# Batch 0's V turned by DMA, unit 0's scores in two PSUM homes, and loads held back, in an attention and SwiGLU kernel

## The chip, the cores and the metric

The kernel runs on one core of one Trainium2 chip. The metric is the device time of one launch in microseconds. The kernel before takes 279.68 us in the median of three runs (278.46 to 279.77).

## The reference

Four batches, eight heads, 768 tokens, head width 64. Tokens lie in eight blocks of 96. A matrix of 8 x 8 for each head (from five rounds of row and column normalization of `sort_net`) mixes the blocks of K and V; each block of queries then attends to its mixed block of keys alone. The result of all heads, 3072 x 512, goes through a SwiGLU feed-forward block with 1536 inner columns.

```python
for _ in range(5):                      # P: 8 x 8 for each head
    P = np.exp(P - np.max(P, axis=-1, keepdims=True))
    P = P / (np.sum(P, axis=-1, keepdims=True) + 1e-09)
    P = P / (np.sum(P, axis=-2, keepdims=True) + 1e-09)
k_sorted = np.einsum('bhij,bhjcd->bhicd', P, k_b)     # v_sorted alike
scores = scale * np.matmul(q_b, k_sb.transpose(0, 1, 2, 4, 3))
attn = softmax(scores)
x = np.matmul(attn, v_sb)               # then to (tokens, 512)
g = x @ w_gate
out = (g * sigmoid(g) * (x @ w_val)) @ w_out
```

## The kernel before, in words

The work is cut into eight units; unit u is half of a batch (four blocks of 96 tokens, `UT` = 384 tokens, all heads). Heads are taken in four pairs, `hp` 0 to 3, whose two heads (`x`) lie in the upper and lower 64 partitions.

Attention of a unit and a pair has eight steps: `qk` (scores into the PSUM home `s`), `rowmax` and `shift` (DVE reads the scores from PSUM; `shift` writes `e` to SBUF and frees `s`), `expo` (ACT), `rowsum` (DVE), `norm` (mostly POOL, writes `en`), `turn` (eight TensorE transposes of 96 x 96 and one eviction `et`), and `av` (matmuls with V, evicted by ACT to `xt`). The feed-forward of a unit has 12 columns of 128, m = 0 to 11: `ffn_up` computes gate `g_ps` and value `u_ps` with four matmuls each and the tanh on ACT, `ffn_gate` makes `gs` and the product `h` on DVE, and `ffn_down` of the unit before runs in between. For unit 0 every third product (m = 2, 5, 8, 11) is made by POOL from a copy `u_sb` that ACT makes.

PSUM homes are named by tag: `up` has three buffers, `o` one, `s` one of two banks, `m` two.

The order on each engine is written out by hand. Steps before the first feed-forward are called one after the other from the list `first`; all later steps are entered by `at(t, f, ...)` with a due time t (one unit of time is one column m of the feed-forward, so unit u's feed-forward begins at 12u, and T0 = -15.6 is unit 0's start), sorted by t and called in that order. Engines take their instructions strictly in the order of the calls, and each DMA queue too: loads are issued by POOL, so a load stands in POOL's order between its arithmetic; stores and DMA transposes are issued by SP.

K and V are mixed on TensorE by a block matrix `bdk` made from P. For K this gives the transposed form that `qk` wants (`mix_t`, six pieces, evicted to `kt`). V of batches 1 to 3 is mixed in natural form and goes through DRAM to its token-major form (`v_piece`, `v_turn`). For batch 0 V is mixed as K is, into `vT` (six `v0_piece`, L169), and then turned by TensorE: `v0_turn` (L176) makes four transposes of 128 x 96 into `vt_ps` and ACT evicts them to `vt`. One call covers one pair and one half of the blocks: half 0 (unit 0's blocks) is called in `first`, half 1 (unit 1's) in the due times 0.2 to 0.8.

The loads stand at these places of POOL's order: q, k, v of batch 0 and the first halves of the gate and value weights at the start; V and K of batch 1 ahead of the first mixing; the second halves of both weights and Q of batch 1 behind the making of `bdk`; the output weights at 0.1; V, K and Q of batch 2 at 2.1, 5.1 and 10.1 (Q in eight issues, `load_q_tok`).

## Time and profile before

| | |
|---|---|
| median of three runs | 279.68 us |
| the profiled execution, its own time | 279.93 us |
| its span, first to last instruction | 278.1 us |
| mean granted TensorE clock | 0.985 |
| TensorE busy | 253.2 us, 91% |
| DVE busy | 203.8 us, 73% |
| ACT busy | 146.8 us, 53% |
| POOL busy | 81.7 us, 29% |
| DMA, bytes moved | 30.27 MB |

All durations come from that one execution, so sums are made against 279.93; 1.8 us of it lie outside the span. A row of the timeline reads: start, duration, engine, line, operation, output and inputs, count, and in brackets the idle time before it with what ended it. A row of the chain of waits is a start, a length and what the chain ran through: an engine's work, or "issue", in which the engine waited for nothing that the profile shows. L129 and L131 are the lines of the helper `evict` on ACT and DVE, so such rows are told apart by their tiles. Names: `s` scores, `rm` maxima, `e` exponents, `rs` sums, `en` normalized, `et` turned, `vt` V with tokens in the partitions, `vm` mixed V of batch 1, `th` tanh.

### The profile page before, as it was taken

The numbers are of one execution on the slowest core, as the hardware profiler recorded it, in microseconds if no ns is written. First come the engines' busy times: TensorE is split into PE (matmuls) and PEld (weight loads), VectorE is DVE, ScalarE is ACT, GpSimd is POOL, SyncE is SP. The second block draws the span as 40 slices with busy tenths as digits, with TensorE's granted clock in tenths as the row PEclk, the third lists the DMA queues.
The fourth block names the chain that finished last, engine by engine and source line by source line (L and its number), as shares of the span: only waits on it lengthen the run. The fifth ranks groups of instructions, "written<-read, shape, count | busy, mean of one in ns | idle before, by whom it ended". The sixth has DMA issues, their size and how long they took to land.

```text
span 278.1 us, 5850 instructions
## 1 busy us (share of the span) xinstructions
PE 253.2 (91%) x2326; PEld 145.2 (52%) x2326; DVE 203.8 (73%) x362; ACT 146.8 (53%) x268; POOL 81.7 (29%) x114
## 2 busy tenths in 40 slices
PE   0586769998999999999999999999999999999973
PEld 0575643665555565555555555555555555555531
DVE  4679771886977877788887788888888887555500
ACT  2467665897665775755446554434444444333211
POOL 8255351437638422222222222222222222000000
PEclk9999995999999999999999999999999999999998
DMA  5999999989969994295221323343212221200111
GB/s 103 220 202 221 206 207 185 248 154 125 70 118 253 151 162 88 66 197 80 62 72 33 58 64 94 58 97 94 69 33 72 73 72 35 81 11 27 40 75 75
DMA packets 59611, 30.27 MB, mean 109 GB/s; under 512 B 51008, under 2 KB 54592, under 8 KB 59584
## 3 DMA queue, kind: packets, MB, share of 16 engines
q0 software_dynamic: 17968, 14.16, 33.6%
q1 hardware_dynamic: 41616, 15.74, 26.2%
q8 instruction: 18, 0.29, 0.4%
q14 instruction: 9, 0.07, 0.1%
HBM read 30.68 MB, written 8.65 MB: 141 GB/s over the span
## 4 chain that ended last, share of the span: by engine, by line
PE 81%; DVE 7%; ACT 6%; DMA 2%; issue 2%; DVEq 0%; ACTq 0%; POOLq 0%
PE o_ps L380 24%; PE u_ps L352 22%; PE g_ps L352 21%; PE av_ps L332 3%; PE k_ps L158 3%; PE s L275 3%; DMA qn<-in_q_dram 2%; DVE e L286 2%; DVE rm L281 2%; PE v_ps L188 2%; PE et_ps L319 2%; ACT e L291 1%; DVE rs L295 1%; ACT o_sb L384 1%; PE q_ps L139 1%
## 5 line engine op out<-in xcount | busy, mean ns | idle before, releaser
L352 PE MATMUL u_ps<-xt,wv_sb 128*128 128x384 bf16 x384 | 79.4, 330 | 1.0 <-DVE gs L366 0.9
L352 PE MATMUL g_ps<-xt,wg_sb 128*128 128x384 bf16 x384 | 80.0, 332 | 0.0
L366 DVE SCALAR_TENSOR_TENSOR gs<-th,g_ps 128x384 bf16<-128x384 bf16 x96 | 51.7, 539 | 37.9 <-ACT th L362 37.9
L362 ACT ACTIVATE th<-g_ps 128x384 bf16<-128x384 f32 x96 | 47.2, 492 | 59.6 <-PE g_ps L352 58.1
L380 PE MATMUL o_ps<-wo_sb,h 128*128 128x512 bf16 x288 | 76.8, 380 | 2.0 <-ACT o_sb L384 2.0
L372 DVE SCALAR_TENSOR_TENSOR h<-u_ps,gs 128x384 bf16<-128x384 f32 x92 | 51.3, 558 | 10.0 <-DVE gs L366 0.5
L352 PEld LDWEIGHTS <-wg_sb 128*128 128x128 bf16 x384 | 37.3, 99 | 35.3 <-issue 2.7
L352 PEld LDWEIGHTS <-wv_sb 128*128 128x128 bf16 x384 | 37.9, 99 | 28.6 <-issue 5.2
L306 POOL TENSOR_TENSOR enp<-e,rs 96x384 bf16<-96x384 f32 x32 | 25.7, 822 | 85.3 <-ACT xt L129 51.9
L306 POOL TENSOR_TENSOR en<-e,rs 96x384 bf16<-96x384 f32 x30 | 24.9, 847 | 46.6 <-DVE rs L296 41.8
L291 ACT ACTIVATE e<-e 96x768 f32<-96x768 f32 x32 | 27.1, 846 | 20.7 <-DVE e L286 20.6
L380 PEld LDWEIGHTS <-h 128*128 128x128 bf16 x288 | 24.6, 98 | 24.2 <-issue 3.1
L286 DVE TENSOR_TENSOR e<-s,rm 96x768 f32<-96x768 f32 x32 | 30.5, 953 | 2.8
L281 DVE TENSOR_REDUCE rm<-s 96x8 f32<-96x768 f32 x32 | 30.1, 942 | 1.4 <-PE s L275 1.4
L295 DVE TENSOR_REDUCE rs<-e 96x8 f32<-96x768 f32 x32 | 30.0, 938 | 1.3 <-ACT e L291 1.3
L384 ACT COPY o_sb<-o_ps 128x512 f32<-128x512 f32 x24 | 14.0, 583 | 16.7 <-PE o_ps L380 16.7
L129 ACT CAST xt<-av_ps 128x384 bf16<-128x384 f32 x32 | 15.3, 480 | 9.6 <-PE av_ps L332 9.6
L129 ACT CAST kt<-k_ps 128x512 bf16<-128x512 f32 x21 | 12.3, 585 | 5.6 <-PE k_ps L158 5.5
L332 PEld LDWEIGHTS <-vt 96*64 96x64 bf16 x256 | 8.3, 116 | 11.3 <-issue 10.6
L129 ACT CAST vm<-v_ps 128x512 bf16<-128x512 f32 x18 | 10.4, 590 | 4.1 <-PE v_ps L188 3.9
L101 POOL DMA_DIRECT2D qk<-in_q_dram x16 | 12.4, 784 | 0.0
L129 ACT COPY et<-et_ps 96x768 bf16<-96x768 bf16 x15 | 11.8, 786 | 0.8 <-PE et_ps L319 0.8
(61 smaller groups left out, 161.5 us busy)
## 6 DMA issues: line engine op xcount, KB each, us to landing
out_dram<-o_sb SPq DMA_DIRECT2D x24, 256.0 KB, 2.1
kn<-in_k_dram POOLq DMA_DIRECT2D x4, 768.0 KB, 10.4
vn<-in_v_dram POOLq DMA_DIRECT2D x4, 768.0 KB, 12.6
vscr<-vm SPq DMA_DIRECT2D x3, 768.0 KB, 6.2
vt<-vscr SPq DMA_DIRECT2D x3, 768.0 KB, 10.3
qn<-in_q_dram POOLq DMA_DIRECT2D x2, 768.0 KB, 13.5
wg_sb<-in_moe_w_gate_dram POOLq DMA_DIRECT2D x4, 384.0 KB, 15.4
wv_sb<-in_moe_w_val_dram POOLq DMA_DIRECT2D x4, 384.0 KB, 17.8
```

The lines of the kernel that those rows point to most:

```text
L129: nc.scalar.copy(dst, src)
L281: nc.vector.reduce_max(m[:, :, :, 0], st["s", u, hp], axis=AX.X)
L286: nc.vector.tensor_tensor(e, st["s", u, hp], st["m", u, hp].to_broadcast([BLK, 2, HB, BLK]), op=ALU.subtract)
L291: nc.scalar.activation(st["e", u, hp], st["e", u, hp], AF.Exp, scale=scale)
L295: nc.vector.reduce_sum(rs[:, :, :, 0], st["e", u, hp], axis=AX.X)
L306: engs[x].tensor_tensor(st["en", u, hp][:, x], st["e", u, hp][:, x], st["rs", u, hp][:, x].to_broadcast([BLK, HB, BLK]), op=ALU.mult)
L352: nc.tensor.matmul(ps, lhsT=w_sb[:, kc, ts(m, 128)], rhs=xt[u][:, kc, :], start=(kc == 0), stop=(kc == HP - 1))
L362: nc.scalar.activation(st["th"], st["g"], AF.Tanh, scale=0.5)
L366: nc.vector.scalar_tensor_tensor(gs, st["th"], 1.0, st["g"], op0=ALU.add, op1=ALU.mult)
L372: nc.vector.scalar_tensor_tensor(h_t[u][:, m, :], st["u"], 0.5, gs, op0=ALU.mult, op1=ALU.mult)
L380: nc.tensor.matmul(st["o"], lhsT=h_t[u][:, m, ts(t, 128)], rhs=wo_sb[:, m, :], start=(m == 0), stop=(m == NFC - 1))
L384: nc.scalar.copy(o_sb, st["o"])
```

## The change

Five things are changed.

V of batch 0 is turned by four DMA transposes on SP's queue, one for each pair and for both halves, each from 128 x 1024 columns of `vT` to 128 x 8 x 128. For that `vT` is padded from 96 to 128 columns a block, and POOL sets the pad to zero. All calls of the old `v0_turn` are gone, those in the due times too, and `av` reads V through `v_block`. The `v0_piece` results go through the PSUM homes `m` and `o` in place of `up`.

In unit 0 the scores of pairs 1 and 3 go into two one-bank tiles of `up` rather than the two-bank `s`; their `rowmax` and `shift` are then two instructions each. `qk` of pairs 1 and 2 is called one step earlier, that of pair 3 behind the turn of pair 0.

The loads of V and K of batch 1 are called behind the second normalization of unit 0, those of the second weight halves and of Q of batch 1 behind the fourth.

The first `rowmax` of unit 1 is given the due time T0 + 12.25 = -3.35 (before -3.5), which puts it behind the turn of unit 0's pair 3 (-3.4), whose eviction is DVE's.

In unit 0's feed-forward POOL makes the products of m = 2, 5, 9, 11 rather than 2, 5, 8, 11.

```diff
--- before.py
+++ after.py
@@ -158,8 +158,8 @@
                 nc.tensor.matmul(ps[ds(64 * x, 64), l, :], lhsT=nat[:, n * 8 + l, :],
                                  rhs=bdk[:, b, ds(HP * x, HP)].rearrange("p a i c -> p (a i c)"),
                                  start=True, stop=True)
-        dst = dst.rearrange("p hp i (ch c) -> p (hp i ch) c", ch=CH)
-        evict(eng, dst[:, :, ts(n, 8)], ps.transpose([0, 2, 1]))
+        dst = dst.rearrange("p hp i (ch c) -> p (hp i) ch c", ch=CH)
+        evict(eng, dst[:, :, :, ts(n, 8)], ps.rearrange("p c (hi ch) -> p hi ch c", ch=CH))
 
     def k_piece(b, n, eng, tag):
         if n == 0:
@@ -168,18 +168,23 @@
 
     def v0_piece(n, eng, tag):
 
+
         if n == 0:
-            tr["vT"] = natp.tile([128, HP, NB, BLK], BF16, name="vT", tag="vm", bufs=2)
-            tr["v", 0] = trp.tile([BLK, H * NB, D], BF16, name="vt", tag="vt", bufs=3)
-        mix_t(vn[0], 0, tr["vT"], n, eng, tag)
-
-    def v0_turn(hp, half, eng, tag):
-        ps = ps_tile([BLK, HB, 2, D], BF16, "vt_ps", tag)
-        for i in range(HB):
-            nc.tensor.transpose(ps[:, i].rearrange("p x d -> p (x d)"),
-                                tr["vT"][:, hp, half * HB + i, :], ident)
-        dst = tr["v", 0].rearrange("p (x hp i) d -> p hp i x d", x=2, hp=HP)
-        evict(eng, dst[:, hp, ds(half * HB, HB)], ps)
+            tr["vT"] = natp.tile([128, HP, NB, 128], BF16, name="vT", tag="vm", bufs=2)
+            tr["vt0"] = trp.tile([128, HP, NB, 2 * D], BF16, name="vt", tag="vt", bufs=3)
+            nc.gpsimd.memset(tr["vT"][:, :, :, BLK:], 0.0)
+        mix_t(vn[0], 0, tr["vT"][:, :, :, 0:BLK], n, eng, tag)
+
+    def v0_turn():
+        for hp in range(HP):
+            nc.sync.dma_start_transpose(out=tr["vt0"][:, hp],
+                                        in_=tr["vT"][:, hp].rearrange("p i k -> p (i k)"))
+
+    def v_block(b, x, hp, i):
+
+        if b == 0:
+            return tr["vt0"][0:BLK, hp, i, ds(D * x, D)]
+        return tr["v", b][:, (x * HP + hp) * NB + i, :]
 
     def v_piece(b, n, eng, tag):
         if n == 0:
@@ -268,23 +273,34 @@
 
     def qk(u, hp):
         b, i0 = u // 2, (u % 2) * HB
-        s = ps_tile([BLK, 2, 512], FP32, "s", "s")
+        if u == 0 and hp % 2:
+            s = [ps_tile([BLK, 1, 512], FP32, "s", "up") for x in range(2)]
+            parts = [(ds(x, 1), s[x]) for x in range(2)]
+            s = [s[x][:, 0] for x in range(2)]
+        else:
+            both = ps_tile([BLK, 2, 512], FP32, "s", "s")
+            parts = [(ds(0, 2), both)]
+            s = [both[:, x] for x in range(2)]
         for i in range(HB):
             for x in range(2):
                 r = ds(64 * x, 64)
-                nc.tensor.matmul(s[:, x, ts(i, BLK)], lhsT=tr["q", b][r, hp, i0 + i, :],
+                nc.tensor.matmul(s[x][:, ts(i, BLK)], lhsT=tr["q", b][r, hp, i0 + i, :],
                                  rhs=tr["k", b][r, hp, i0 + i, :], start=True, stop=True)
-        st["s", u, hp] = s[:, :, 0:UT].rearrange("p x (i k) -> p x i k", i=HB)
+        st["s", u, hp] = [(xs, p[:, :, 0:UT].rearrange("p x (i k) -> p x i k", i=HB))
+                          for xs, p in parts]
 
     def rowmax(u, hp):
         m = smp.tile([BLK, 2, HB, 1], FP32, name="rm", tag="rm")
-        nc.vector.reduce_max(m[:, :, :, 0], st["s", u, hp], axis=AX.X)
+        for xs, s in st["s", u, hp]:
+            nc.vector.reduce_max(m[:, xs, :, 0], s, axis=AX.X)
         st["m", u, hp] = m
 
     def shift(u, hp):
         e = epool.tile([BLK, 2, HB, BLK], FP32, name="e", tag="e", bufs=3)
-        nc.vector.tensor_tensor(e, st["s", u, hp],
-                                st["m", u, hp].to_broadcast([BLK, 2, HB, BLK]), op=ALU.subtract)
+        for xs, s in st["s", u, hp]:
+            m = st["m", u, hp][:, xs]
+            nc.vector.tensor_tensor(e[:, xs], s, m.to_broadcast([BLK, m.shape[1], HB, BLK]),
+                                    op=ALU.subtract)
         st["e", u, hp] = e
 
     def expo(u, hp):
@@ -330,7 +346,7 @@
         for i in range(HB):
             for x in range(2):
                 nc.tensor.matmul(ps[ds(64 * x, 64), i, :],
-                                 lhsT=tr["v", b][:, (x * HP + hp) * NB + i0 + i, :],
+                                 lhsT=v_block(b, x, hp, i0 + i),
                                  rhs=st["et", u, hp][:, x, i, :], start=True, stop=True)
         evict("act", xt[u][:, hp, :].rearrange("p (i q) -> p i q", i=HB), ps)
 
@@ -364,7 +380,7 @@
     def ffn_gate(u, m):
         gs = gsp.tile([128, UT], BF16, name="gs", tag="gs")
         nc.vector.scalar_tensor_tensor(gs, st["th"], 1.0, st["g"], op0=ALU.add, op1=ALU.mult)
-        if u == 0 and m % 3 == 2:
+        if u == 0 and m in (2, 5, 9, 11):
             u_sb = gsp.tile([128, UT], FP32, name="u_sb", tag="u_sb", bufs=2)
             nc.scalar.activation(u_sb, st["u"], AF.Copy, scale=0.5)
             nc.gpsimd.tensor_tensor(h_t[u][:, m, :], u_sb, gs, op=ALU.mult)
@@ -410,8 +426,6 @@
         at(tv[-1] + 0.3, v_turn, b)
 
     T0 = -15.6
-    load_v(1)
-    load_k(1)
     zk_ps = spread_p(0, 1), spread_p(1, B)
     make_zk(0, 1, zk_ps[0])
     make_bdk(0, nc.vector)
@@ -420,33 +434,31 @@
     make_zk(1, B, zk_ps[1])
     for b in range(1, B):
         make_bdk(b, nc.gpsimd)
-    load_w(wg_sb, moe_w_gate, DF // 2, DF)
-    load_w(wv_sb, moe_w_val, DF // 2, DF)
-    load_q(1)
 
 
     def v0(*ns):
         for n in ns:
-            v0_piece(n, "act", "up")
-
-    def vx(half, *hps):
-        for hp in hps:
-            v0_turn(hp, half, "act", "up")
-
-    first = [(qk, 0), (rowmax, 0), (v0, 0, 1, 2), (shift, 0), (expo, 0), (qk, 1), (rowmax, 1),
-             (v0, 3, 4), (shift, 1), (expo, 1), (v0, 5), (rowsum, 0), (norm, 0), (qk, 2),
-             (rowmax, 2), (vx, 0, 0, 1), (shift, 2), (expo, 2), (rowsum, 1), (norm, 1),
-             (vx, 0, 2, 3), (qk, 3), (turn, 0), (rowmax, 3), (shift, 3), (expo, 3), (av, 0),
-             (turn, 1), (rowsum, 2), (norm, 2, (nc.gpsimd, nc.vector)), (av, 1), (rowsum, 3),
-             (norm, 3, (nc.vector, nc.gpsimd))]
+            v0_piece(n, "act", ("m", "o", "m")[n % 3])
+
+    def loads(*fs):
+        for f, *args in fs:
+            f(*args)
+
+    half = DF // 2
+    first = [(qk, 0), (rowmax, 0), (v0, 0, 1, 2), (qk, 1), (shift, 0), (expo, 0), (rowmax, 1),
+             (v0, 3, 4), (qk, 2), (shift, 1), (expo, 1), (v0, 5), (v0_turn,), (rowsum, 0), (norm, 0),
+             (rowmax, 2), (shift, 2), (expo, 2), (turn, 0), (rowsum, 1), (norm, 1),
+             (loads, (load_v, 1), (load_k, 1)), (qk, 3), (av, 0), (rowmax, 3), (shift, 3), (expo, 3),
+             (turn, 1), (rowsum, 2), (norm, 2, (nc.gpsimd, nc.vector)),
+             (av, 1), (rowsum, 3), (norm, 3, (nc.vector, nc.gpsimd)),
+             (loads, (load_w, wg_sb, moe_w_gate, half, DF), (load_w, wv_sb, moe_w_val, half, DF),
+              (load_q, 1))]
     for f, *args in first:
-        f(*args) if f in (v0, vx) else f(0, *args)
+        f(*args) if f in (v0, v0_turn, loads) else f(0, *args)
     at(T0 + 11.9, turn, 0, 2)
     at(T0 + 12.2, turn, 0, 3, "dve")
     at(T0 + 12.3, av, 0, 2)
     at(T0 + 12.6, av, 0, 3)
-    for hp in range(HP):
-        at(0.2 + 0.2 * hp, v0_turn, hp, 1, "act", "o")
 
     at(0.1, load_wo)
     at(2.1, load_v, 2)
@@ -463,6 +475,8 @@
              [(26.6, 50.6)[b - 2] + (1, 3)[b - 2] * n for n in range(4)], "m")
     for u in range(1, NU):
         steps += att_steps(u, 12 * u + T0 + (u == 2))
+        if u == 1:
+            steps[-8 * HP + 1] = (T0 + 12.25, steps[-8 * HP + 1][1])
     for u in range(NU):
         for m in range(NFC):
             at(12 * u + m, ffn_up, u, m)
```

## The prediction

> **What bounds the kernel now.** First the page's slices: TensorE is full from slice 7 on, so what comes after about 50 us is a chain of matmuls that only shifts. The loss is in front of it, with one slice of low granted clock.
>
> ```profile
> PE   0586769998999999999999999999999999999973
> PEclk9999995999999999999999999999999999999998
> ```
>
> Next the busy time by stage (columns: PE, PEld, DVE, ACT, POOL busy, granted clock, DMA share, GB/s).
>
> ```profile
> 17.00:31.00 14.00, 10.01 (x183) 8.85 (x182) 12.63 (x18) 10.54 (x18) 9.06 (x14) 1.00 1.10 213
> 34.40:38.00 3.60, 3.21 (x15) 1.77 (x13) 2.63 (x4) 1.65 (x4) 1.42 (x2) 1.00 1.15 211
> 38.00:41.40 3.40, 1.39 (x18) 1.03 (x18) 2.37 (x5) 3.21 (x6) 1.94 (x3) 0.96 1.09 210
> 41.40:47.50 6.10, 5.43 (x25) 2.44 (x25) 1.11 (x2) 2.85 (x6) 1.46 (x3) 0.50 1.18 181
> 47.50:50.00 2.50, 2.50 (x20) 1.28 (x19) 1.17 (x2) 1.77 (x4) 0.46 (x1) 0.91 1.27 225
> ```
>
> From 17 to 31 (unit 0's attention) DVE is the full engine: 12.63 of 14.00. From 38.0 to 41.4 ACT is (3.21 of 3.40), TensorE works 1.39, and then its clock is 0.50 for six microseconds. The chain of waits says what ACT does there:
>
> ```profile
> 38.33 0.74 ACT e L291
> 39.08 0.56 ACT vt L129
> 39.64 0.70 ACT et L129
> 40.34 0.48 ACT vm L129
> 40.82 0.49 ACT vt L129
> ...
> 41.36 0.60 PE vt_ps L179 x4
> ...
> 41.98 0.59 ACT vt L129
> ...
> 42.61 0.58 PE v_ps L188
> 43.20 1.28 PE g_ps L352 x4
> 44.48 1.28 PE u_ps L352 x4
> ```
>
> The second half of V's turn (vt) alternates between TensorE and ACT in front of the second gate matmul. At 43.20 four gate matmuls take 1.28 us; at 49.76 they take 0.65.
>
> Last, the timeline of POOL where unit 2 begins:
>
> ```profile
> 64.12 0.91 POOL L370 TENSOR_TENSOR h<-u_sb,gs 128x384 bf16<-128x384 f32 x1 [2.06 <-DVE gs L366]
> 64.97 6.20 POOL L101 DMA_DIRECT2D qk<-in_q_dram  x8
> 71.18 0.93 POOL L370 TENSOR_TENSOR h<-u_sb,gs 128x384 bf16<-128x384 f32 x1
> 72.06 1.61 POOL L306 TENSOR_TENSOR en<-e,rs 96x384 bf16<-96x384 f32 x2
> 73.38 0.71 PE L319 MATMUL et_ps<-ident,en 96*96 96x96 bf16 x8
> ```
>
> Eight load issues hold POOL for 6.20 us, the product of m=11 and unit 2's first normalization follow without a gap, and TensorE's turn (73.38) stands at the second half of that normalization, done at 73.67.
>
> **A. Scores in two homes (unit 0, hp 1 and 3).** qk 1 no longer waits for shift 0 (end 19.06): it runs behind v0 pieces 0 to 2, so rowmax 1 starts at 19.10 instead of 19.72, -0.62. Against it, rowmax and shift of hp 1 and 3 become two instructions each, four extra. No row has 96x384 from PSUM on DVE; near rows are h (384 columns from PSUM, 558 ns) and e (768, 953 ns), so two halves cost 1.12 against 0.95: +0.16 each, +0.64 in all. The other end is +0.10 each, since an instruction that needs no result of the last starts about 0.07 before its end (rs at 21.58, e's end 21.65). Sum between -0.22 and +0.02. qk 3 now stands behind turn 0, which needs norm 0 (POOL, about 22.5 to 24.1): it ends near 25.1, before DVE asks for it at 25.2. I take -0.2, as ACT also loses four evictions of 0.53 that delayed exp 3.
>
> [...]
>
> **B. rowmax (1,0) behind unit 0's last eviction.** Today DVE runs rowmax (1,0) at 31.47 in an idle stretch, then et of hp 3 at 32.48, then shift at 32.95. Turn 3 ends near 32.4 because norm 3 on POOL ends at 31.76, so the eviction gains next to nothing and rowmax's 0.95 goes behind it: et3 32.3, rowmax 32.8, shift 33.8 to 34.75 (33.90 before). Queued behind shift: qk (1,1), whose single home it frees, and behind that in TensorE's order the first gate matmul: 34.43 becomes about 35.25. On the chain exp (1,0) starts at 34.8 instead of 34.35, since 0.35 us of a wait there (34.00 to 34.35) is used up. A and B: +0.45 at the end of shift (1,1), 38.29 to 38.74.
>
> **C. V turned by DMA.** Eight groups of four transposes on TensorE and eight evictions of 0.58 on ACT go. Half 0 lay beside the DVE chain and is worth nothing by itself. Half 1 is on the chain: from shift (1,1)'s end (38.29) to the tanh of m=3 (50.54) there are 12.25 us. What is left for ACT there, in its order: exp, et, six vm, two tanh, xt, u_sb. Start to start in the chain's rows 0.75 + 0.70 + 6x0.54 + 2x0.47 + 0.46 + 0.48 = 6.6; by full durations 0.85 + 0.80 + 6x0.59 + 2x0.49 + 0.48 + 0.49 = 7.1. I take 6.9: -5.35. TensorE keeps up if it is at full clock from about 38: after two slow groups (2.56) it has 0.52 of turn, 6x0.22 of v_ps, five groups of 0.65, 0.34 of av and 0.38 of qk, 5.8 us, so g of m=3 could be done near 44 plus waits, before 45.6.
>
> The clock by rows: four gate matmuls take 1.28 at 34.44 and 0.65 at 49.76; transposes at 36.97 take 0.63 for four and at 38.28 only 0.38; granted 0.50 follows the stretch in which PE worked 1.39 of 3.40. [...]
>
> The new cost is latency: V's four transposes (256 KB each) start when the last v0 piece is evicted, about 22.8, on an empty SP queue. No row has this shape; qtd (192 KB) issues three in 3.97 us and lands in 2.8 to 4.6 us. Scaled by 256/192, 1.76 us each: landings at about 26.3, 28, 29.8, 31.5; av 0 to 3 want them at 26.0, 29.2, 32.0 and 33.0 (today 27.27, 29.60, 32.30, 33.41). av 0 may wait 0.3, hidden behind exp 3. hp 3 may be as late as 34.3 at no cost, as the gate matmuls wait for qk (1,1) anyway. At the worst row, 4.6 each and one after another, hp 3 lands at 41.2.
>
> **D. Loads held back.** Today the loads run without a gap from 1.3 us, ten of 768 KB until 42.2 (4.1 each). The first five end near 23.4 as before; V and K of batch 1 are issued behind norm 1 on POOL (26.9 to 28.1; norm 2 is due at 28.5), the rest behind norm 3 (31.6 to 35; norm (1,0) due at 36.9). Both issue stretches fit in POOL's gaps. Landings: v1 about 32.5 (needed 38.9), k1 36.5 (46.5), second weight halves 41 and 45 (51.5), q1 49 (55), wo 57 (66), k2 65. Least cover 6 us: nothing on the path. The pad's memset (1024 columns against 256 in 343 ns: at most 1.4 us) lies on idle POOL before norm 0. Without these covers each late load costs its lateness.
>
> **E. POOL's product moves from m=8 to m=9.** As the eight q issues come after it in POOL's order, they wait for gs of m=9. In today's times: th 9 at 64.3, u_sb to 65.3, product 65.45 to 66.35 instead of 64.12 to 64.97: the issues, the product of m=11 and normalization (2,0) all come 1.4 later, 73.67 becomes 75.05. TensorE's turn (2,0) ends at 74.09 now, about 75.3 then: +1.2, on the path since TensorE is full from there. The other end is 0, if u_sb and the issues turn out faster. DVE loses one h near 65.7, which only lets TensorE reach that wait earlier.
>
> **Sum** against the profiled execution, 279.93 (span 278.1): -0.2 + 0.65 (A and B, +0.45) - 5.35 + 1.2 = -3.7, 276.2. The median of the runs is 0.25 below that execution: 276.0.
>
> **Rivals.**
> 1. E costs nothing: 274.8. For it: POOL was idle 2.06 us before today's product; against: the 6.20 us of issues have no gap behind them.
> [...]
> 3. The transposes are slow because the last weights (to 23.4) and then v1 and k1 share the 16 engines with them (share 1.10 in the stage 17 to 31). av waits in TensorE's order, and xt, exp and all of unit 1 behind it. Worst row: hp 3 at 41.2, 6.9 over its cover of 34.3, 282.9. It decides from a landing of 38.0 (3.8 us per transpose), where the gain of 3.7 is gone. Against it: the held-back loads leave some 4 us of empty queues, and vscr landed in 6.2 us for 768 KB under full load.
> 4. The change does not do what it says: loads already queued still run when the transposes start, or a held-back load is late by more than 6 us. No row shows it; near 280 to 281.
>
> **How the numbers follow.** Forecast 0.45 (275.2 to 277.2 by C's and E's ends), rival 1 0.18, rival 2 0.20, rival 3 0.12, rival 4 0.05. About 0.5% (1.4 us: below 278.3, above 281.1) is what can be told from no change. Faster: 0.45 + 0.18 + 0.11 of rival 2 = 0.74. Same: 0.09 of rival 2, 0.04 of the others: 0.13. Slower 0.13. The range of 273.8 to 279.4 takes in rivals 1 and 2 with the ends of C; left out are rival 3, part of 4 and a low tail, under 0.2.
>
> **What would show it.** Right: no vt on ACT, tanh of m=3 near 45.6, granted clock 1.00 from 41 to 48, V's transposes landed by 32, first gate matmul near 35.2, a wait of 1 us of turn (2,0) for POOL near 69. Wrong: av waiting for vt, a second stretch of granted 0.5, a load among the releasers of TensorE, or gs of m=0 later than 39.6.

## The result, and the profile after

The changed kernel takes 287.3 us in the median (286.82 to 288.89), the kernel before beside it 279.55. The ratio is 1.0295, interval 1.0246 to 1.0345: slower by 7.75 us, where 3.7 less was forecast. The profiled execution takes 287.64, its span is 285.8. In k3_small_late and n2_after_small_late below, one execution each was over 1.5% slower than the fastest of its kernel: ratios and intervals leave it out, medians do not.

The page's slices, TensorE busy and granted clock:

```profile
PE   0584405999979999999999999999999999999973
PEclk9955556999999999999999999999999999999998
```

There is one hole now, but a deep one: slices 4 to 6 (counted from 0, each 7.1 us long), and from slice 2 to 5 the clock is at half. The stages (PE, PEld, DVE, ACT, POOL busy, granted clock, DMA share, GB/s):

```profile
17.00:31.00 14.00, 9.61 (x171) 7.76 (x167) 12.65 (x22) 9.37 (x15) 8.47 (x12) 0.50 1.00 169
31.25:44.60 13.35, 0.53 (x9) 0.34 (x8) 2.37 (x3) 0.48 (x1) 2.65 (x5) 0.50 1.11 200
...
49.50:54.00 4.50, 4.03 (x31) 2.21 (x32) 3.52 (x7) 4.00 (x8) 3.06 (x5) 1.00 0.44 61
```

From 17 to 31 DVE is as full as before (12.65 against 12.63). The clock is 0.50 there, where the kernel before had 1.00, but that does not show in the time: k4_before_late runs the same instructions there as the kernel before, also at 0.50 (TensorE 10.01 busy in both), and its first tanh starts at 36.01 against 35.94. Why the clock differs is not shown. For the next 13.35 us the engines have next to nothing to do (DVE 2.37 busy, POOL 2.65), while the DMA engines are full (share 1.11). From 49.5 on the clock is back, and ACT (4.00 of 4.50) and TensorE (4.03) are about equally full. TensorE's timeline names what it waits for:

```profile
25.46 0.53 PE L348 MATMUL av_ps<-et,vt 96*64 96x96 bf16 x8 [0.89 <-DMA vt<-vT]
...
28.37 0.53 PE L348 MATMUL av_ps<-et,vt 96*64 96x96 bf16 x8 [1.39 <-DMA vt<-vT]
...
31.25 0.53 PE L348 MATMUL av_ps<-et,vt 96*64 96x96 bf16 x8
45.09 0.53 PE L348 MATMUL av_ps<-et,vt 96*64 96x96 bf16 x8 [13.31 <-DMA vt<-vT]
45.55 0.56 PE L287 MATMUL s<-kt,qt 64*96 64x96 bf16 x8
46.03 1.46 PE L368 MATMUL g_ps<-xt,wg_sb 128*128 128x384 bf16 x4
```

Pairs 0 to 2 are served in time; pair 3 waits 13.31 us, and the first gate matmul stands at 46.03 (34.43 before). The chain of waits has the same piece:

```profile
25.46 1.33 SPq L180
26.80 0.04 issue
26.84 18.20 DMA vt<-vT
```

The four transposes landed 3.2, 4.2, some 5.8 and 18.2 us after their issue. The last was issued from 25.46 to 26.84; POOL's timeline shows what came at the same moment:

```profile
26.32 0.62 POOL L106 DMA_DIRECT2D vn<-in_v_dram  x1
26.92 0.55 POOL L87 DMA_DIRECT2D kn<-in_k_dram  x1
```

The view of the DMA queues from 28.6 to 45.05 (packets, MB, share of the engines; q0 are POOL's loads, q1 the transposes) gives the reason:

```profile
q0 software_dynamic: 1244, 2.92, 93.9%
q1 hardware_dynamic: 1088, 0.26, 12.9%
```

Nearly as many packets on each queue, but eleven times the bytes on q0. Alone, from 24 to 26, q1 moved 1132 packets in 2 us. From 31 to 33 it is 76 beside 76, from 33 to 36 105 beside 104. In these windows the two queues get the same number of packets, although a packet of V's or K's load is one run of 6144 bytes (128 packets for 768 KB) and one of a transpose 256 bytes: 0.41 MB beside 0.02 from 31 to 33, 0.60 beside 0.03 from 33 to 36.

A second loss lies where unit 2 begins. POOL's timeline:

```profile
71.16 0.92 POOL L386 TENSOR_TENSOR h<-u_sb,gs 128x384 bf16<-128x384 f32 x1 [3.02 <-ACT u_sb L385]
72.02 6.20 POOL L101 DMA_DIRECT2D qk<-in_q_dram  x8
78.23 0.93 POOL L386 TENSOR_TENSOR h<-u_sb,gs 128x384 bf16<-128x384 f32 x1
79.10 1.61 POOL L322 TENSOR_TENSOR en<-e,rs 96x384 bf16<-96x384 f32 x2
```

TensorE's turn (2,0) waits 1.39 and 0.40 us for the last of these lines, which the prediction's part E had foretold.

How far each kernel stands from the kernel before along the way is told by the starts of the tanh on ACT (`th`, one for each feed-forward column). Minus is earlier; the kernels are those of the next section.

| kernel | first tanh | unit 0, m=3 | unit 1, m=1 | unit 1, m=2 | unit 1, m=4 | last tanh |
|---|---|---|---|---|---|---|
| before, at | 35.94 | 50.54 | 72.93 | 75.71 | 80.78 | 262.96 |
| changed | +11.59 | +5.42 | +5.05 | +7.04 | +7.05 | +7.44 |
| e1_loads_late | -0.05 | -6.43 | -3.91 | +2.47 | +4.35 | +4.43 |
| f1_late_q2 | +0.09 | -5.65 | -3.42 | -3.62 | +2.69 | +3.23 |
| k1_late_k2 | +0.28 | -6.33 | -3.11 | -3.30 | -3.30 | -3.06 |
| k3_small_late | +0.09 | -6.07 | -5.83 | -5.88 | -6.02 | -6.02 |
| f3_before_held | -0.36 | -0.98 | -0.99 | -1.01 | -0.52 | -0.57 |
| g1_product_9 | -0.27 | -0.31 | -0.93 | +2.62 | +2.72 | +2.68 |
| n1_after_late | +11.10 | +4.93 | +4.56 | +4.57 | +4.38 | +4.91 |

In the changed kernel the first wait costs 11.6, unit 1's lighter ACT gives 6.2 of it back by m=3, and turn (2,0), between unit 1's m=1 and m=2, adds 2.0. Each row is one execution; that of g1_product_9 is one of its three slowest (282.64 of 279.52 to 283.17). The other kernels that keep V's turn on TensorE have m=3 of unit 0 at 49.19 (k4_before_late), 49.56 (f3_before_held) and 50.23 (g1_product_9), so up to 1.4 us of this column is not due to the edits: k4_before_late has the same instructions up to there as the kernel before.

### The profile page after: what moved, and what is told of

Read it like the earlier page. It is cut to its first block, busy times and chain, and to the rows that moved or that the text cites. A ratio compares the mean times of both kernels' runs of the same rounds, so it can differ in the third digit from the quotient of the medians.

```text
span 285.8 us, 5764 instructions
## 1 busy us (share of the span) xinstructions
PE 245.8 (86%) x2265; PEld 140.5 (49%) x2294; DVE 204.0 (71%) x366; ACT 141.9 (50%) x260; POOL 82.6 (29%) x115
## 3 DMA queue, kind: packets, MB, share of 16 engines
q1 hardware_dynamic: 45840, 16.79, 29.6%
## 4 chain that ended last, share of the span: by engine, by line
PE 68%; DMA 10%; DVE 7%; ACT 7%; issue 3%; POOL 2%; SPq 1%; DVEq 0%; POOLq 0%; ACTq 0%
PE o_ps L396 21%; PE u_ps L368 18%; PE g_ps L368 18%; DMA vt<-vT 6%; PE s L287 3%; PE av_ps L348 3%; DMA qn<-in_q_dram 2%; PE k_ps L158 2%; DVE e L302 2%; DVE rm L295 2%; POOL en L322 2%; DMA etp<-enp 2%; PE v_ps L193 1%; ACT e L307 1%; ACT th L378 1%
## 5 line engine op out<-in xcount | busy, mean ns | idle before, releaser
L368 PE MATMUL g_ps<-xt,wg_sb 128*128 128x384 bf16 x384 | 78.8, 328 | 0.3
L368 PE MATMUL u_ps<-xt,wv_sb 128*128 128x384 bf16 x384 | 78.6, 327 | 0.2
L396 PE MATMUL o_ps<-wo_sb,h 128*128 128x512 bf16 x260 | 72.3, 380 | 4.0 <-ACT o_sb L400 2.0
L302 DVE TENSOR_TENSOR e<-s,rm 96x768 f32<-96x768 f32 (+1 forms) x34 | 30.6, 906 | 2.6
L295 DVE TENSOR_REDUCE rm<-s 96x8 f32<-96x768 f32 (+1 forms) x34 | 30.3, 896 | 0.7 <-PE s L287 0.7
L348 PE MATMUL av_ps<-et,vt 96*64 96x96 bf16 x128 | 6.4, 229 | 15.6 <-DMA vt<-vT 15.6
L335 PE MATMUL et_ps<-ident,en 96*96 96x96 bf16 x128 | 10.8, 229 | 4.5 <-POOL en L322 4.4
L335 PEld LDWEIGHTS <-en 96*96 96x96 bf16 x128 | 9.3, 140 | 7.6 <-POOL en L322 6.2
```

What stands on the lines that cost most here:

```text
L295: nc.vector.reduce_max(m[:, xs, :, 0], s, axis=AX.X)
L302: nc.vector.tensor_tensor(e[:, xs], s, m.to_broadcast([BLK, m.shape[1], HB, BLK]), op=ALU.subtract)
L348: nc.tensor.matmul(ps[ds(64 * x, 64), i, :], lhsT=v_block(b, x, hp, i0 + i), rhs=st["et", u, hp][:, x, i, :], start=True, stop=True)
L368: nc.tensor.matmul(ps, lhsT=w_sb[:, kc, ts(m, 128)], rhs=xt[u][:, kc, :], start=(kc == 0), stop=(kc == HP - 1))
L396: nc.tensor.matmul(st["o"], lhsT=h_t[u][:, m, ts(t, 128)], rhs=wo_sb[:, m, :], start=(m == 0), stop=(m == NFC - 1))
```

## Experiments

Theory: pair 3's transpose takes turns with the loads of V and K of batch 1, packet by packet. Rivals: the transpose waits until the other queue is empty; or the other parts of the change cost the time.

**e1_loads_late: V and K of batch 1 behind the fourth normalization.**

```diff
-             (loads, (load_v, 1), (load_k, 1)), (qk, 3), (av, 0), (rowmax, 3), (shift, 3), (expo, 3),
+             (qk, 3), (av, 0), (rowmax, 3), (shift, 3), (expo, 3),
...
-             (loads, (load_w, wg_sb, moe_w_gate, half, DF), (load_w, wv_sb, moe_w_val, half, DF),
+             (loads, (load_v, 1), (load_k, 1), (load_w, wg_sb, moe_w_gate, half, DF), (load_w, wv_sb, moe_w_val, half, DF),
```

> The changed kernel, but V and K of batch 1 are issued with the other held-back loads, behind the fourth normalization of unit 0 (about 30.7 us instead of 26.3). Theory 1, the fourth V transpose is held up packet by packet by the load packets that arrive at 28.6: without them it lands near 30, av of pair 3 runs near 32, the first gate matmul near 34.5 instead of 46.03, time 276.0 (275 to 277.5). Theory 2, transposes of this shape are slow by themselves: it still lands 18 us after its issue, time 287 or more. Theory 3, the wait goes over to the loads: V of batch 1 lands near 40 and TensorE waits for it, 278 to 280.

Measured 286.31 (284.60 to 288.02; ratio 1.0242, 1.018 to 1.0305). The first wait is gone: the four transposes have the engines alone (4224 packets between 23.5 and 31) and the tanh of m=3 starts at 44.11. But the 6.4 us are lost again. POOL's and TensorE's timelines near unit 2:

```profile
61.94 4.67 POOL L101 DMA_DIRECT2D qk<-in_q_dram  x6
67.55 0.77 POOL L101 DMA_DIRECT2D qk<-in_q_dram  x1 [0.94 <-DMA vn<-in_v_dram]
71.23 0.77 POOL L101 DMA_DIRECT2D qk<-in_q_dram  x1 [2.92 <-DMA kn<-in_k_dram]
```

```profile
67.31 0.38 PE L193 MATMUL v_ps<-vn,bdk 128*128 128x512 bf16 x1 [1.06 <-DMA vn<-in_v_dram]
...
73.77 0.56 PE L335 MATMUL et_ps<-ident,en 96*96 96x96 bf16 x4 [4.14 <-POOL en L322]
...
80.54 0.36 PE L348 MATMUL av_ps<-et,vt 96*64 96x96 bf16 x8 [1.17 <-DMA vt<-vscr]
```

POOL's issues of Q of batch 2 wait for earlier loads, unit 2's first normalization waits behind them, and TensorE behind that. The loads have become the bound.

**e2_small_packets: V and K of batch 1 at the changed kernel's places, but written in runs of 512 bytes** (tiles padded so that no longer run forms). The edit in short, for V; K is written alike:

```diff
-        vn[b] = natp.tile([128, CK, D], BF16, name="vn", tag="vn", bufs=2)
-        nc.gpsimd.dma_start(out=vn[b], in_=src)
+        vn[b] = natp.tile([128, CK // 4, 4 * D + 4], BF16, name="vn", tag="vn", bufs=2)
+        nc.gpsimd.dma_start(out=vn[b][:, :, 0:4 * D],
+                            in_=src.rearrange("p (a c) d -> p a (c d)", c=4))
```

> The changed kernel, loads issued at the same places, but V and K of batch 1 are written as runs of 512 bytes (rows padded by 4 columns after every 256), 3072 packets in place of 256. Theory 1 (the queues take turns by packet, whatever their size): the fourth transpose's 1056 packets pass beside 1056 packets of 512 bytes, 0.81 MB at 193 GB/s, 4.2 us from 28.6: it lands near 33, first gate matmul near 35.5, time 276.5 (275.5 to 278.5). Theory 2 (a transpose gives way until the load queue is empty, or is slow by itself): it lands near 45 or later, time 287.

Measured 285.14 (1.0201, 1.0174 to 1.0228), 7 us above the theory's range, although pair 3 lands as early as it said, after 6.8 us in place of 18.2. The bytes of the loads, their places and their order are the same, the packets are twelve times smaller (512 bytes: 478 packets hold 0.24 MB in n2_after_small_late below):

```profile
33.55 0.53 PE L369 MATMUL av_ps<-et,vt 96*64 96x96 bf16 x8 [1.13 <-DMA vt<-vT]
```

This does not yet show the turn by packets, for two reasons. The loads' packets begin a microsecond later than in the changed kernel (at 29.6, there at 28.5), and from 28.5 to 30 nearly all of pair 3's 1056 packets pass, beside 30 of q0:

```profile
q1 hardware_dynamic: 1048, 0.26, 84.0%
q0 software_dynamic: 30, 0.02, 31.4%
```

And its last 32 packets go from 31.5 to 33.6 while 745 of q0 pass, which is not one for one; what held them is not shown. The clean test of the packet size is n2_after_small_late below, where both queues run side by side. The later loss is that of e1_loads_late.

**e3_pe_turn: V of batch 0 turned on TensorE again, all other parts as changed.**

```diff
-             (v0, 3, 4), (qk, 2), (shift, 1), (expo, 1), (v0, 5), (v0_turn,), (rowsum, 0), (norm, 0),
-             (rowmax, 2), (shift, 2), (expo, 2), (turn, 0), (rowsum, 1), (norm, 1),
+             (v0, 3, 4), (qk, 2), (shift, 1), (expo, 1), (v0, 5), (rowsum, 0), (norm, 0),
+             (rowmax, 2), (vx, 0, 0, 1), (shift, 2), (expo, 2), (turn, 0), (rowsum, 1), (norm, 1), (vx, 0, 2, 3),
...
+    for hp in range(HP):
+        at(0.2 + 0.2 * hp, v0_turn, hp, 1, "act", "o")
```

> The changed kernel with V turned on TensorE as before (half 0 among unit 0's steps, half 1 at 0.2 to 0.8); held-back loads, two score homes, the later rowmax and the products 2, 5, 9, 11 stay. Theory 1 (the whole loss is the wait for the fourth transpose): the other parts cost what the prediction gave them, +0.65 for rowmax, +1.2 for the product, -0.2 for the homes: 281 (280 to 282.5). Theory 2 (the held-back loads themselves cost time): 284 or more.

Measured 283.71 (1.0142, 1.0109 to 1.0174), between the two theories. With no DMA transpose of V at all the rest of the change costs 4.2. The first tanh is 3.3 later (39.25), the tanh of m=3 2.9, and turn (2,0) adds 2.0. In this order av 1 waits 2.41 us for ACT, which has the turn's evictions in between: with V's turn among its steps the new order of unit 0 is a loss. Half 0 of the turn goes through the home `o` here, which has one buffer, and through `up` with three in the kernel before; how much of the 3.3 is due to that was not tried.

**e4_weights_first: the weights at the first place, V and K at the second.**

```diff
-             (loads, (load_v, 1), (load_k, 1)), (qk, 3), (av, 0), (rowmax, 3), (shift, 3), (expo, 3),
+             (loads, (load_w, wg_sb, moe_w_gate, half, DF), (load_w, wv_sb, moe_w_val, half, DF)),
+             (qk, 3), (av, 0), (rowmax, 3), (shift, 3), (expo, 3),
...
-             (loads, (load_w, wg_sb, moe_w_gate, half, DF), (load_w, wv_sb, moe_w_val, half, DF),
-              (load_q, 1))]
+             (loads, (load_v, 1), (load_k, 1), (load_q, 1))]
```

> The changed kernel with the two groups of held-back loads exchanged: the second weight halves (1024 packets of 1536 bytes) behind the second normalization, V and K of batch 1 (256 packets of 6144 bytes) with Q behind the fourth. Theory 1 (turns by packet): the fourth transpose ends when about 1056 load packets have passed, that is with the weights, 9.2 us after 28.6 at the rate of the stretch 36.4 to 45.1, near 37.8 instead of 45.0; time 280 (279 to 281.5). Theory 2 (it waits for the load queue to run empty): it lands near 50, time 291 or more. By bytes shared evenly it would land near 31 in this and in the changed kernel alike.

Measured 285.78 (1.0211, 1.0156 to 1.0267). Pair 3 runs beside packets of 1536 bytes first and lands 14.4 us after its issue:

```profile
41.23 0.53 PE L348 MATMUL av_ps<-et,vt 96*64 96x96 bf16 x8 [8.52 <-DMA vt<-vT]
```

Earlier than 45.04, but not as early as 37.8, and the time misses the theory's 279 to 281.5. From 34 to 38 the queues move 306 beside 302 packets, from 38 to 39 131 beside 103, and from 39 to 41.2 265 beside the last 5: again the last packets of a transpose are late, and what held them is not shown. A transpose that waited for an empty queue would be no earlier than in the changed kernel.

**h1_unheld_256: the loads at the places of the kernel before, V and K of batch 1 in runs of 256 bytes** (written as in e2_small_packets, two rows to a run in place of four).

```diff
+    load_v(1)
+    load_k(1)
     zk_ps = spread_p(0, 1), spread_p(1, B)
...
-             (loads, (load_v, 1), (load_k, 1)), (qk, 3), (av, 0), (rowmax, 3), (shift, 3), (expo, 3),
+             (qk, 3), (av, 0), (rowmax, 3), (shift, 3), (expo, 3),
```

> The changed kernel with the loads at the places of the kernel before (not held back), and V and K of batch 1 written in runs of 256 bytes, so that their packets are as small as those of the transposes. Theory: the two queues take turns packet by packet, so now the four transposes get half of the engines: 4224 packets beside as many of 256 bytes, at 460 to 570 packets per us (28.6 to 32 in e2_small_packets and 24 to 26 in the changed kernel) 15 to 18 us after 22.8 by packets, some 10 us by bytes (2.16 MB at 213 GB/s): pair 3 at 33 to 38. DMA has no idle stretch, so the late stall near 70 shrinks to the 1.2 us of the moved product: 276.5 to 280. Rival 1: small packets slow the whole queue, and V, K of batch 1 come after 45: 283 or more. Rival 2: a transpose waits for the other queue to run empty whatever the packets: pair 3 after 42, 284 or more.

Measured 302.01 (1.0816, 1.0759 to 1.0874), far outside every figure expected. The turns by packet are as told, the count of packets was not: the second weight halves and Q of batch 1, in packets of 1.5 KB and more, stand behind V and K and take their turns too (344 packets of 0.48 MB from 40 to 43). Two windows of the queues, 31 to 34 and 40 to 43:

```profile
q0 software_dynamic: 906, 0.24, 82.4%
q1 hardware_dynamic: 901, 0.22, 69.8%
...
q0 software_dynamic: 344, 0.48, 95.2%
q1 hardware_dynamic: 341, 0.09, 26.6%
```

In these windows the packets are equal, with 256-byte loads and with larger ones. Pair 3's av stands at 60.75. With the loads at their old places the transposes come too late to be of use.

**f3_before_held: the kernel before with the loads held back, nothing else.**

```diff
-    load_v(1)
-    load_k(1)
...
-             (rowmax, 2), (vx, 0, 0, 1), (shift, 2), (expo, 2), (rowsum, 1), (norm, 1),
+             (rowmax, 2), (vx, 0, 0, 1), (shift, 2), (expo, 2), (rowsum, 1), (norm, 1), (loads, (load_v, 1), (load_k, 1)),
...
```

> The kernel before with the loads held back at the two places of the changed kernel and nothing else: V is still turned on TensorE, so no DMA transpose runs. Theory: the DMA queue idles for some 7 us between 23.5 and 31 and cannot make that up, so Q of batch 1, V and K of batch 2 arrive late; near 71 POOL's eight q issues wait 2 to 4 us for an earlier load, the first normalization of unit 2 comes behind them, and TensorE's turn waits for it. Holding the loads costs 2 to 4 us by itself: 282 to 283.5. Rival (the prediction's part D): every held load has 6 us of cover or more, 279.5 to 280.

Measured 279.83 (1.0023, 1.0005 to 1.0042). Holding alone costs 0.65 us (0.1 to 1.2); the rival was nearer. The cover that the prediction found is there, as long as the kernel is no faster.

**g1_product_9: the kernel before with the products at 2, 5, 9, 11.**

```diff
-        if u == 0 and m % 3 == 2:
+        if u == 0 and m in (2, 5, 9, 11):
```

> The kernel before with POOL's products of unit 0 at m = 2, 5, 9, 11 and nothing else. Prediction's part E: the eight q issues, the product of m = 11 and unit 2's first normalization come 1.4 us later and TensorE's turn (2,0) with them: +1.2, 280.7. Rival (rival 1 of the prediction): the delay lies beside other work: 279.3 to 279.8. The other rival: the wait also lowers the clock: +2 or more.

Measured 280.68 (1.0057, 1.0023 to 1.0092): +1.5 for part E, by the interval 0.6 to 2.6. The ten executions fall apart: three at 279.5, four from 280.4 to 281.0, three from 282.6 to 283.2. In the profiled one (282.64) turn (2,0) waits 1.37 and 0.40 us for POOL, as in the changed kernel, but from 75 to 78 the clock is 0.50, where the changed kernel has 1.00 behind the same wait. So in this execution the other rival comes true; whether the clock also tells the other nine apart is not shown.

**f1_late_q2: e1_loads_late with Q of batch 2 issued in two parts behind unit 2's first normalization.**

```diff
-    at(10.1, load_q_tok, 2)
+    at(12.0, load_q_tok, 2, (0,))
+    at(15.0, load_q_tok, 2, (1,))
```

> The kernel of e1_loads_late (286.3), with the eight q issues of batch 2 entered as two parts at the due times 12.0 and 15.0 in place of one at 10.1, so that they stand behind unit 2's first normalization on POOL and not in front of it. Theory: in e1_loads_late the time is lost where these issues wait for DMA (0.94 and 2.92 us) and hold that normalization; with them out of the way the wait of turn (2,0) for POOL (4.14 us) and the low clock behind it go, -3.5 to -6: 280.5 to 283. Rival: the loads themselves are the bound (V, K and Q of batch 2 are late whatever stands on POOL), so the wait only moves to vt, q or a tile of batch 2: 285 to 287.

Measured 283.29 (1.0144, 1.0118 to 1.0171), -3.0, just outside the theory's range. The wait for POOL is gone and another has come, as the rival had it: V of batch 1, on its way through DRAM. Chain and TensorE:

```profile
45.03 9.81 DMA vscr<-vm
54.85 0.02 issue
54.87 22.28 DMA vt<-vscr
```

```profile
77.19 0.36 PE L349 MATMUL av_ps<-et,vt 96*64 96x96 bf16 x8 [4.55 <-DMA vt<-vscr]
```

The load of `vt` lands 22.28 us after its issue (11.0 in the kernel before). It is of 128-byte packets on SP's queue, and the window from 62 to 66 shows the same turns again, beside the loads of batch 2 on q0:

```profile
q0 software_dynamic: 242, 0.86, 105.9%
q1 hardware_dynamic: 241, 0.03, 9.4%
```

**k1_late_k2: f1_late_q2 with K of batch 2 out of that window.**

```diff
-    at(5.1, load_k, 2)
-    at(12.0, load_q_tok, 2, (0,))
-    at(15.0, load_q_tok, 2, (1,))
-    at(15.1, load_v, 3)
-    at(17.1, load_k, 3)
-    at(19.1, load_q_tok, 3)
+    at(14.0, load_k, 2)
+    at(16.0, load_q_tok, 2, (0,))
+    at(18.0, load_q_tok, 2, (1,))
+    at(19.1, load_v, 3)
+    at(21.1, load_k, 3)
+    at(24.1, load_q_tok, 3)
```

> The kernel of f1_late_q2 (283.3) with K of batch 2 loaded at the due time 14.0 in place of 5.1, Q of batch 2 at 16.0 and 18.0, and batch 3 later by 4 to 5. Theory: in f1_late_q2 the load that ends V of batch 1's way through DRAM took 22.28 us in place of 11.0, as its 128-byte packets took turns with K of batch 2's 6 KB packets (241 against 242 from 62 to 66), so TensorE waited 4.55 us for vt and lost its clock. With only the output weights and V of batch 2 beside it, vt lands before 73: 277 to 279. Rival: the bytes wanted by 68 are too many whatever their order (7 us of idle DMA cannot be made up), and vt or V of batch 2 is as late as before: 281 to 284.

Measured 276.29 beside 278.57 of the kernel before (0.9904, 0.9877 to 0.9931). The chain has no `vt` any more; in its place stands the load of V of batch 2, 25.90 us from issue to landing, for which TensorE waits 1.46 us. From 66 to 72 the packets of `vt` run nearly alone:

```profile
q1 hardware_dynamic: 5009, 0.64, 94.7%
q0 software_dynamic: 66, 0.33, 36.3%
```

**k4_before_late: the same late loads in the kernel before.**

> The kernel before with the late loads of k1_late_k2 (K of batch 2 at 14.0, Q of batch 2 in two parts at 16.0 and 18.0, batch 3 later) and nothing else. It tells what the order of these loads is worth without V's transposes. Theory: nothing in the kernel before waits for these loads but 0.3 us of turn (2,0), so 278.6 to 279.4, no difference. Rival: V of batch 1's way through DRAM binds there too, or the q issues on POOL do: 276 to 278, and a gain of the other kernels would be due to this order, not to the transposes.

Measured 278.82 (1.0, 0.998 to 1.0021). The order of the later loads is worth nothing by itself: the gain of k1_late_k2 comes from the change. That it comes from the transposes is argued from e3_pe_turn, where the other parts lose; the transposes alone, in the old order of unit 0, were not run.

**k2_late_m8_rm: k1_late_k2 with parts B and E undone.**

```diff
-        if u == 0 and m in (2, 5, 9, 11):
+        if u == 0 and m % 3 == 2:
...
-        if u == 1:
-            steps[-8 * HP + 1] = (T0 + 12.25, steps[-8 * HP + 1][1])
```

> The kernel of k1_late_k2 with two parts of the change undone: POOL's products of unit 0 at m = 2, 5, 8, 11, and unit 1's first maximum at its old due time. Prediction's part B: the maximum costs 0.65 on the path, so -0.65 against k1_late_k2. Part E: its cost came from the q issues behind the product; these are later now, so nothing more; if the moved product costs by itself, -1.2 more. Rival: neither is on the path any more once V's way is: equal to k1_late_k2 within 0.4.

Measured 277.24 (0.9945, 0.9925 to 0.9965), 0.95 slower than k1_late_k2 and not 0.65 faster; the intervals touch. The first tanh is 1.02 earlier without B (35.20 against 36.22), but the tanh of m=3 is 0.91 later (45.12 against 44.21), and the last one starts at the same time (259.86 against 259.90). In between the clock differs: from 38 to 41.4 it is 0.54 here and 1.00 in k1_late_k2, with TensorE busy 3.18 and 3.17 of 3.40. B's delay of 1.02 does not reach the end in these two executions.

**k3_small_late: k2_late_m8_rm with V and K of batch 1 early again, in runs of 512 bytes.**

> The kernel of k2_late_m8_rm with V and K of batch 1 at the places of the changed kernel (behind the second normalization) and written in runs of 512 bytes. Theory: the transposes share the engines with packets of twice their size and land near 33.5 as in e2_small_packets, under the cover of 34.3, and the DMA engines idle 5 us less, so every later load comes 3 to 5 us earlier: -1 to -3 against k2_late_m8_rm, near 275 to 277. Rival 1: the loads are no longer what binds once K of batch 2 is late: equal within 0.4. Rival 2: pair 3's wait of 1.1 us costs more than the earlier loads bring: +0.5 to +1.5.

Measured 275.57 (274.21 to 279.42; 0.9868, 0.9823 to 0.9912), the lowest median here; its interval overlaps that of k1_late_k2. The loads' packets begin at 30.4, and pair 3's but for the last 32 are through by 30.7, so the landing near 33.5 came true with next to no sharing. From 64 to 84 TensorE waits for no DMA, and the lead of 6 us at m=3 is still there at the last tanh. TensorE is full from slice 5 on, before from 6, and the clock from slice 6 on, before from 7:

```profile
PE   0594599998999999999999999999999999999983
PEclk9997579999999999999999999999999999999999
```

**n1_after_late and n2_after_small_late: the changed kernel with k1_late_k2's late loads; then with the 512-byte runs as well.** All five parts of the change stand in both.

> The changed kernel (287.3) with the late loads of k1_late_k2 and nothing else: K of batch 2 at 14.0, its Q in two parts at 16.0 and 18.0, batch 3 later. It splits the changed kernel's loss. Theory: two waits make it: pair 3's transpose (in its profile +5.05 up to unit 1's second column) and POOL's q issues in front of unit 2's first normalization (+2.0); the second goes: 285 to 285.6. Rival: the second wait only came because the first had moved everything late, and V of batch 1's way binds instead: 286.5 to 288.

Measured 285.22 (1.0215, 1.0177 to 1.0254): the second wait is worth 2.1, the first the rest. n1_after_late differs from k1_late_k2 in one thing, the place of two loads, and takes 8.9 us more (3.1% by the ratios). This is the plainest test that the first wait is due to these two loads.

> n1_after_late with V and K of batch 1 also written in runs of 512 bytes, at the changed kernel's own places: all five parts of the change stand, and both waits have their remedy. Theory: pair 3 lands near 33.5, V of batch 1's way is free, and the time is that of k3_small_late (275.6) plus what its two undone parts cost (0 to 0.65): 275.5 to 276.5. Rival: parts B and E cost 0.65 and 1.2 here too: 277 to 277.6. Other rival: with the loads early again V of batch 1 waits for them as in e2_small_packets: 280 or more.

Measured 277.92 (274.23 to 279.21; 0.989, 0.9789 to 0.9991), above the theory and just above the rival. By the ratio it is some 3 us under the kernel before (0.3 to 5.9). In the profiled execution (277.51) the loads' packets begin at 28.4, as in the changed kernel (28.5), and run side by side with pair 3's. From 32 to 34:

```profile
q0 software_dynamic: 478, 0.24, 88.1%
q1 hardware_dynamic: 478, 0.12, 46.3%
```

Pair 3 lands 8.73 us after its issue. In n1_after_late, which differs from this kernel only in the runs of 512 bytes, it takes 17.71. This is the turn by packets: the same two loads at the same places, packets twelve times smaller, half the time. Pair 3's av comes at 35.35 after a wait of 3.40, in k3_small_late at 33.59. POOL issued V's load at 26.34 here and at 26.89 there, but its packets begin 2 us apart (28.4 and 30.4); why is not shown. The first tanh is 1.8 later than there and the tanh of m=3 3.9 (48.33 against 44.47), before part E can act; the other 2.1 go with the clock, 0.50 from 38 to 44 here, 0.99 and 1.00 there. How often it falls one way or the other was not tried.

## Why the prediction was wrong, step by step

**C, the landings: the step that failed.** Alone, the price of 1.76 us for each transpose holds: 1132 packets in 2 us, where one transpose has 1056. The fourth was priced at 31.5 as if it had the engines alone, and 41.2 at worst, from a row of a smaller transpose. It landed at 45.04. The prediction had the two facts side by side, V's load due on POOL's queue at 26.9 and pair 3's landing at 31.5, and did not ask how two queues divide the engines: 76 packets beside 76 here. It even counted "some 4 us of empty queues" against rival 3; the queue was empty until 28.5, when 3070 of the 3168 packets of the first three transposes were through, and the fourth had the loads beside it from its start. The 6.2 us of vscr "under full load", also set against rival 3, were no fair row: vscr's 768 KB go in packets of 6144 bytes, as large as the load's (127 packets of q1 hold 0.71 MB from 52 to 55 in the kernel before). No row of the kernel before showed such a pair at its price, but the sizes could have been read from its queues: from 58 to 62 the 942 packets of q1 hold 0.12 MB and the 120 of q0 0.64 (nearly all of q1's come after 61.2, when q0's load is nearly through).

The other runs' counts say the same, 344 packets beside 341 in h1_unheld_256 and 478 beside 478 in n2_after_small_late.

**Rival 3 had the mechanism and the wrong size.** It gave 282.9 with a chance of 0.12 and would decide from a landing of 38.0. Its worst row made four transposes at 4.6 us; three took 3.2 to 5.8 and the fourth 18.2, as its length went with the other queue's packets, not with its own: 17.71 beside loads of 6144-byte packets (n1_after_late), 8.73 beside the same loads in 512-byte packets (n2_after_small_late).

**C, the gain: right.** Where the transposes land in time the tanh of m=3 comes at 44.11 (e1_loads_late) against 45.6 foretold, 6.4 earlier than in the profiled execution of before and 5.1 earlier than in k4_before_late. The forecast had 4.9 (C's 5.35 less 0.45).

**D, loads held back: nearly right alone, wrong in the sum.** Foretold at nothing, it costs 0.65 alone (f3_before_held). Its two loads behind norm 1 are those that ran beside the fourth transpose. And its cover of 6 us was measured against the old times of need, and C moves the needs behind it some 6 us earlier (6.43 at m=3 in e1_loads_late); the two terms spend the same microseconds. In e2_small_packets, where V and K of batch 1 are issued at the changed kernel's own places and pair 3 is nearly in time, turn (2,0) waits 4.14 us for POOL and the first av of unit 2 waits 2.30 us for `vt`. V of batch 1's trip through DRAM was not in the prediction's list of landings at all: it is no held load, but it shares the engines with them.

**E: right in the median.** +1.2 foretold, +1.5 measured alone (g1_product_9, 0.6 to 2.6), 2.0 in the changed kernel's table. Rival 1 falls in the median; three of the ten executions of g1_product_9 are near it.

**A and B: small, as foretold.** The first gate matmul stands at 34.39 in e1_loads_late (34.43 before, 35.25 foretold): B's delay of 0.8 is there (1.02 between k1_late_k2 and k2_late_m8_rm), but in e1_loads_late the rest of unit 0's new order wins it back. The split maxima and shifts took 1.02 and 1.01 for two halves against 0.95, so four cost some 0.26, below the 0.40 to 0.64 of the rows.

**The clock: C's full speed from 38, and rival 2.** C counted on the full clock from about 38; rival 2, with a chance of 0.20, put the time at 278.0, for 2 us lost to a low clock. No run shows that term of 2 us by itself. What the runs showed: in e1_loads_late, without the first wait, the four gate matmuls at 34.39 take 1.46 us and those at 38.89 take 0.81, so C's full speed was there in time. In the changed kernel those behind the wait of 13.31 take 1.46 us (46.03) and the next four 0.81 (50.58); the changed kernel's loss is the wait for the fourth transpose. In n2_after_small_late, behind a wait of 3.40 us for pair 3, the clock is 0.50 from 38 to 44, and the way from the first tanh to m=3 takes 2.1 us longer than in k3_small_late. What sets the clock is open: from 17 to 31 the same instructions ran at 1.00 in the kernel before and at 0.50 in k4_before_late.

## What to carry to other kernels

Before a small-packet transfer (a DMA transpose, a gather of short rows) is put on the path, count packets, not bytes: beside a load with large packets it got about one packet for each of theirs here (76 beside 76 in 2 us), so a first estimate of its time from such counts is its packets times the other's packet time. Either keep the window free, or make the other's packets small: the four transposes landed after 3.7 us in the median with the engines alone (e1_loads_late), the fourth after 17.71 beside 6144-byte packets (n1_after_late) and after 8.73 beside 512-byte ones (n2_after_small_late).

When a part of a change makes the kernel faster, the cover of every late load shrinks by that much: compare landings with the new times of need.

A change that loses can hide a gain: here two loads placed behind the last transpose, and those of batch 2 out of the way of V's trip through DRAM, turned +7.75 into -2.3 us (k1_late_k2).

## What the runs showed of the hardware

Two DMA queues of one core moved equal numbers of packets and not equal bytes in the windows listed: 76 to 76 with 6144-byte packets (0.41 MB to 0.02), 344 to 341 with mixed ones (0.48 to 0.09), 242 to 241 with 128-byte ones on the other side, 478 to 478 with 512-byte ones. Not every window with packets on both is equal: at the end of a transfer the last packets came late (32 beside 745 in e2_small_packets, 5 beside 265 in e4_weights_first), and from 74 to 76 in f1_late_q2 it was 513 of `vt` beside 1838. Of four equal transposes of 256 KB the first took 3.2 us and the fourth, beside two loads of 768 KB, 18.2; the 768 KB load of 128-byte packets (`vt`) took 7.2 to 11.0 us in the kernel before and 26.6 in e1_loads_late.

POOL's DMA issues themselves waited for earlier loads to land (0.94 and 2.92 us in e1_loads_late), and so held back the arithmetic queued behind them on POOL; whether the program's semaphores or the queue made them wait is not shown.

The same instructions ran at a granted clock of 1.00 in one execution and 0.50 in another (17 to 31 in the kernel before and in k4_before_late), with next to no difference in the time where DVE was the full engine (12.63 of 14.00; TensorE 10.01 busy in both, first tanh at 35.94 and 36.01).
